# Fused attention, gated product and sine product on one core: the sine stages in another order

## The chip, the cores and the metric

The kernel runs on one core of a Trainium2 chip. The metric is the device time of one execution in microseconds (us); the time of a kernel is the median of its runs. Five engines with one instruction queue each work side by side: PE (TensorE: matmuls, and PEld, the weight loads that belong to them), DVE (VectorE), ACT (ScalarE), POOL (GpSimd) and SP (SyncE), which here issues the ordinary DMA transfers. An engine executes its instructions in the order in which they stand; where one waits for a semaphore, those behind it wait too.

## The reference

```python
x = attention(q, k, v)            # 4608 tokens x 512, chunks of 64 tokens, softmax within a chunk
x = ((x @ w1) * (x @ w2)) @ w3 @ w_o        # 512 -> 1024 -> 1024 -> 512
h = x @ w_in                      # 512 -> 2048
g = h * np.cos(h)
out = g @ w_out                   # 2048 -> 512, float32
```

All is float32. The kernel multiplies on the 16-bit path of PE: each operand is split in two float16 halves, and a product is made of three matmuls (high by high, low by high, high by low).

## The kernel before

The 4608 tokens are nine blocks of 512 (block 0 to block 8). Until about 730 us the kernel does attention and the gated product, and converts the weights of the sine part to halves that it keeps in DRAM. From there on it runs the **sine stages**, which the change is about: for each block `h_of` (first product, cosine, splitting of g) and `y_of` (second product).

Both products use Strassen's scheme in Winograd's form on 2x2 blocks: seven products in place of eight, with sums of blocks before and after. In `h_of` a block has four groups (`f_` 0 to 3). A group makes seven products (line 1296, 6 matmuls of 128x256 in each of two halves) in three PSUM tiles x, y and z; five PSUM banks serve these in turn. ACT copies a finished PSUM tile to SBUF (`kept`, line 1305), and DVE adds another to it (`plus`, line 1311). That gives four quarters of h: c11 (name hm1), c22 (hv5), c12 (hm3) and c21 (hu2). `finish` makes h cos h of each: two DVE instructions that take off whole turns (1336, 1339), a sine on ACT (1342), a multiplication on DVE (1345). `part` splits a quarter into halves, one instruction on ACT (1317) and one on DVE (1320): these are the operands of the second product. Operands 0, 1 and 2 are c11, c12 and c22 themselves. Operands 5, 3, 4 and 6 are sums, made in this chain: c11 += c21 (operand 5), then c21 += c22 (operand 3), c22 += c11 (operand 4), c12 += c22 (operand 6). Of these `add`s the first and third run on DVE (1330); the second and fourth are, in blocks 0 to 7, transfers that add in flight, which POOL issues (line 1326, 64 in all, 256 KB each). The third add overwrites c22, which the second reads; operand 3 needs the second to have landed, operand 6 the fourth.

`y_of` makes seven terms (line 1393, 12 matmuls for each of the four groups of one term) in three PSUM tiles of their own (psyx, psyy, psyz); line 1408 (ACT) and 1414 (DVE) take them out, line 1420 stores. Each term has its own 1 MB of weights, which SP fetches (line 1261) into one of three buffers; each pair of half groups of `h_of` needs 896 KB fetched in the same way. The second product of block b is interleaved with the first of block b + 1.

The order on every queue comes from a planner (`Plan.order`). It walks through time with a cost per instruction (for instance 0.7 us for an add on DVE), and when an engine is free it takes, of the instructions that are ready, the one with the lowest priority number. A result is ready for another engine at its planned end plus a latency from the table LAT. A transfer ends, in the plan, when its bytes have passed at DMA_RATE behind all earlier ones, and 2.2 us later it has landed. Most instructions of a group of `h_of` have the priority `pr`, the group's start in an even pace; the terms of `y_of` have `prio + i * unit`, i being the term's place. Nothing of the plan is kept at run time but the order: the engines wait for semaphores.

Of the kernel before, what the change touches and what calls it, by code (L numbers as in the profile page):

```python
# [25 lines left out]


MM = 0.2155
LAT = {"PE": 0.35, "DVE": 0.4, "ACT": 0.4, "POOL": 0.5, "SP": 2.2}
DMA_RATE = 380e3  # L30
ROWS = 2.7
AHEAD = 5.0
SHARED = 0.8
ISSUE = {"DVE": 0.9, "ACT": 0.88}
# [25 lines left out]


class Op:
    __slots__ = ("n", "eng", "cost", "prio", "fn", "deps", "succ", "bufs", "allocs", "left", "ready", "start", "size", "alts", "many", "psum")


class Plan:
# [6 lines left out]
        self.ops = []  # L73
        self.touched = {}

    def op(self, eng, cost, prio, fn, r=(), w=(), size=0, after=()):

        o = Op()
        o.psum = any(b.pool is not None and b.pool.places[0][0] == "PS" for b in (x[0] if isinstance(x, tuple) else x for x in r))
        o.many = isinstance(eng, dict)  # L80
        if o.many:
            o.alts, eng = eng, None
        else:
            o.alts = {eng: cost}
        o.alts = {e: c * ISSUE.get(e, 1.0) for e, c in o.alts.items()}
        o.n, o.eng, o.cost, o.prio, o.fn, o.size = len(self.ops), eng, cost, prio, fn, size
        o.deps, o.succ, o.bufs, o.allocs = set(), [], [], []
        norm = [x if isinstance(x, tuple) else (x, None) for x in r], [x if isinstance(x, tuple) else (x, None) for x in w]

        def meets(p, q):  # L90
            return p is None or q is None or p == q

        for b, part in norm[0]:
            assert b.writers, f"{b.name} is read before it is written"
            o.deps.update(x for x, p in b.writers if meets(p, part))
        for b, part in norm[1]:
            o.deps.update(x for x, p in b.writers if meets(p, part))
            o.deps.update(x for x, p in b.readers if meets(p, part))
        for b, part in norm[0]:
            b.readers.append((o.n, part))  # L100
        for b, part in norm[1]:
            if b.first is None:
                b.first = o.n
                if b.pool is not None:
                    o.allocs.append(b)
            b.writers = [(x, p) for x, p in b.writers if not (part is None or p == part)] + [(o.n, part)]
            b.readers = [(x, p) for x, p in b.readers if not (part is None or p == part)]
        for b in {id(b): b for b, _ in norm[0] + norm[1]}.values():
            b.users += 1
            o.bufs.append(b)  # L110
            o.deps.add(b.first)
        o.deps.update(x.n for x in after)
        o.deps.discard(o.n)
        self.ops.append(o)
        return o

    def order(self):
# [9 lines left out]
        left = {}  # L127
# [14 lines left out]
        ends = {}  # L142
# [14 lines left out]
        while done < len(ops):  # L157
# [11 lines left out]
            for e in ENGINES:  # L169
                while pending[e] and pending[e][0][0] <= now + 1e-9:  # L170
                    _, prio, n = heapq.heappop(pending[e])
                    heapq.heappush(waiting[e], (prio, n))
                if free[e] > now + 1e-9 or not waiting[e]:
                    continue
                if e == "SP" and dma > now + AHEAD:
                    heapq.heappush(wakes, dma - AHEAD)
                    continue
                aside, got = [], None
                while waiting[e]:
                    x = heapq.heappop(waiting[e])  # L180
                    o, taken, where = ops[x[1]], [], []
                    if o.start is not None:
                        continue
                    for b in o.allocs:
                        found = place(b, taken)
                        if found is None:
                            break
                        where.append((b, found[0]))
                        taken.append(found[1])
                    else:  # L190
                        got = o
                        for b, k in where:
                            b.place = k
                            if b.pool.queue:
                                b.pool.line.pop()
                        live += taken
                        break
                    aside.append(x)
                for x in aside:
                    heapq.heappush(waiting[e], x)  # L200
                if got is None:
                    continue
                o = got
                o.start, o.eng, o.cost = now, e, o.alts[e]
                if e == "DVE":
                    if not o.psum:
                        o.cost += SHARED * max(0.0, port - now)
                    on_psum = o.psum
                elif e == "POOL" and not o.size:
                    if free["DVE"] > now and not on_psum:  # L210
                        o.cost += SHARED * (free["DVE"] - now)
                    port = now + o.cost
                order.append(o)
                free[e] = now + o.cost
                end = now + o.cost
                if o.size:
                    dma = max(dma, now + o.cost) + o.size / DMA_RATE
                    end = dma
                heapq.heappush(wakes, free[e])
                for s in o.succ:  # L220
                    s.left -= 1
                    there = end if list(s.alts) == [e] and not o.size else end + LAT["SP" if o.size else e]
                    s.ready = max(s.ready, there)
                    if not s.left:
                        for a in s.alts:
                            heapq.heappush(pending[a], (s.ready, s.prio, s.n))
                        heapq.heappush(wakes, s.ready)
                for b in o.bufs:
                    left[id(b)] -= 1
                    ends[id(b)] = max(ends.get(id(b), 0.0), end + LAT["SP" if o.size else e])  # L230
                    if not left[id(b)] and b.pool is not None:
                        heapq.heappush(frees, (ends[id(b)], id(b), b))
                        heapq.heappush(wakes, ends[id(b)])
                done += 1
# [24 lines left out]
def fused_kernel(  # L259
# [33 lines left out]
    scale = 1.0 / math.sqrt(D)  # L293
    KB = 1024

    R0, R1, C0, C1, A0, A1, A2, A3, I0, I1, I2, I3, I4, I5, F0, Y1, Y0 = 0.9, 10.9, 16.5, 27.6, 60.0, 6, 70.0, 10.6, 240.5, 10.0, 28.1, 430.0, 5.6, 11.6, 8.4, 16.0, 8.0

    const = ctx.enter_context(tc.tile_pool(name="const", bufs=1))
    sb = ctx.enter_context(tc.tile_pool(name="sb", bufs=1))
# [157 lines left out]
    with tc.manual_schedule():  # L457
# [819 lines left out]
        def h_of(bl):  # L1277
# [8 lines left out]
            for f_ in range(K2 // 4):  # L1286
# [36 lines left out]
                def add(a, b, way, pr=pr):  # L1323
                    if way:
                        def f():
                            nc.gpsimd.dma_start(a.ap, b.ap, accum_op=ALU.add)
                        op("POOL", 1.2, pr, f, r=[a, b], w=[a], size=2 * P * 2 * KB)
                    else:
                        def f():
                            nc.vector.tensor_tensor(out=a.ap, in0=a.ap, in1=b.ap, op=ALU.add)  # L1330
                        op("DVE", 0.7, pr, f, r=[a, b], w=[a])
# [35 lines left out]
                plus(z, c21)  # L1367
                finish(0, 1, c21)
                way = [bl < NB - 1 and i in (1, 3) for i in range(4)]
                add(c11, c21, way[0])  # L1370
                add(c21, c22, way[1])
                part(5, c11)
                add(c22, c11, way[2])
                part(3, c21)
                add(c12, c22, way[3])
                part(4, c22)
                part(6, c12)

        def y_of(bl):
            tg, last = gh.pop(bl), bl == NB - 1  # L1380
            prio = start_h[bl] + (8 * pair + 20.0 if bl == 0 else period) + Y0
            unit, iy = period / 8, hsc[bl][2]
            x, y, z = (Buf(ps_y[n], f"psy{n}{bl}") for n in "xyz")

            def multiply(ps, a, b, i, more=False):
                w = fetch(bl, b, prio + i * unit - Y1)
                for f_ in range(4):
# [7 lines left out]
                                        start=(not more and f_ == 0 and n == 0 and j == 0 and m == 0), stop=(f_ == 3 and n == 1 and m == 2), skip_group_check=True,  # L1395
                                    )
                    at = prio + i * unit + f_ * unit / 8
                    if last and i in (0, 1, 3):
                        at = prio + (f_ - 4) * 8.0 + i
                    op("PE", 6 * MM, at, f, r=[tg[a, f_], w], w=[ps])  # L1400

            def two(a):
                return a.rearrange("p (j e) -> p j e", j=2)
# [21 lines left out]
            multiply(y, 1, 1, 1)  # L1425
            plus(y, c11, 1)
            store(c11, 0, 0, 1)
            multiply(x, 4, 4, 2, True)
            c21 = kept(x, "u2", 2)
            multiply(z, 5, 5, 3)  # L1430
            multiply(x, 3, 3, 4, True)
            c22 = kept(x, "v5", 4)
            plus(z, c22, 4)
            store(c22, 1, 1, 4)
            multiply(x, 6, 2, 5, True)
            c12 = kept(x, "m3", 5)
            store(c12, 0, 1, 5)
            multiply(z, 2, 6, 6, True)
            plus(z, c21, 6)
            store(c21, 1, 0, 6)  # L1440


        warm = Buf(ps_mm0, "warm")
# [65 lines left out]
```

## Time and profile before

| | |
|---|---|
| median of 3 runs | 1465.75 us (1462.08 to 1469.79) |
| the profiled execution | 1461.54 us |
| its span, first to last instruction | 1459.5 us |
| PE, share of the span | 94% |
| DVE, ACT, POOL | 80%, 66%, 15% |
| DMA, mean | 190 GB/s |

A busy PE is not a PE at its peak: its matmuls overlap, and their ends are modelled. Of an engine's row the number in square brackets is the idle time just before the instruction, with what ended it. The sine stages end with the program. In them a matmul of 128x256 follows the one before it after about 0.11 us if nothing holds it (13.11 us for 120 of them in the last group of rows below).

### The profile page before, as it was taken

The page shows a single profiled execution, that of the slowest core. Times are in us where ns is not written, and L with a number is a line of the kernel's source. Part 1 is how long each engine was busy: PE and PEld are TensorE (multiplying, and loading weights), DVE is VectorE, ACT ScalarE, POOL GpSimd, SP SyncE. Part 2 cuts the span into 40 slices and gives each one's busy share as a digit, 9 for nine tenths or more (in the row PEclk, how much of TensorE's full clock was granted, in tenths as well). Part 3 has the DMA queues.
Part 4 walks back from the last instruction along what each step waited for, and adds up shares of the span by engine and source line. Part 5 has one row for each costly group of instructions (what it writes and reads, how often), then busy time and mean ns, then how long its engine had stood idle before and what let it go on. Part 6 is the DMA issues. An engine that isn't in the chain of part 4 may idle for free. (4 is left out here: it accounts for less than half of the span.)

```text
span 1459.5 us, 32138 instructions
## 1 busy us (share of the span) xinstructions
PE 1378.7 (94%) x12984; PEld 1104.1 (76%) x12984; DVE 1172.3 (80%) x2015; ACT 958.2 (66%) x2090; POOL 224.2 (15%) x193
## 2 busy tenths in 40 slices
PE   5789999999999999999999898999898999999998
PEld 3356767777786868686878787888786888878887
DVE  8789787459989657895589898898878897978893
ACT  4788776769876769886377565656555564655552
POOL 0000114113641212531200000001000000000000
PEclk7999999999999999999999999999999999999999
DMA  9951582237777317635145787868585968777634
GB/s 317 270 113 36 159 275 52 74 76 235 191 232 224 77 54 218 178 91 199 76 154 179 251 262 236 271 222 249 171 302 167 302 195 269 219 248 238 225 131 146
DMA packets 196629, 276.83 MB, mean 190 GB/s; under 512 B 121216, under 2 KB 151936, under 8 KB 187264
## 3 DMA queue, kind: packets, MB, share of 16 engines
q1 hardware_dynamic: 187264, 257.99, 54.9%
q0 software_dynamic: 9216, 16.78, 6.5%
q8 instruction: 102, 1.67, 0.5%
q14 instruction: 47, 0.39, 0.1%
HBM read 224.40 MB, written 33.55 MB: 177 GB/s over the span
## 5 line engine op out<-in xcount | busy, mean ns | idle before, releaser
L978 PE MATMUL ps<-XHL,W 128*128 128x256 f16 x3024 | 347.1, 273 | 6.2 <-ACT RES L485 5.0
L1296 PEld LDWEIGHTS <-ATT 128*128 128x128 f16 x3024 | 297.1, 98 | 51.8 <-issue 14.7
L978 PEld LDWEIGHTS <-W 128*128 128x128 f16 x3024 | 292.6, 98 | 45.5 <-issue 7.4
L1393 PE MATMUL ps<-CONV,W 128*128 128x256 f16 x2304 | 278.0, 275 | 24.7 <-DVE W L1320 9.5
L1393 PEld LDWEIGHTS <-W 128*128 128x128 f16 x2304 | 225.6, 98 | 57.5 <-DVE W L1320 11.9
L1296 PE MATMUL ps<-XHL,ATT 128*128 128x256 f16 x1632 | 198.6, 274 | 6.2 <-ACT WG L1305 2.2
L1342 ACT ACTIVATE RES<-RES,quarter 128x512 f32<-128x512 f32 x144 | 102.9, 717 | 98.0 <-DVE RES L1339 97.8
L485 ACT ACTIVATE RES<-ps,smalls 128x512 f32<-128x512 f32 x126 | 87.2, 699 | 55.4 <-PE ps L978 50.4
L998 DVE SCALAR_TENSOR_TENSOR RES<-ps,smalls,RES 128x512 f32<-128x512 f32 x108 | 80.1, 746 | 45.0 <-ACT RES L485 25.4
L1088 PE MATMUL ps<-WG 128*128 128x512 f16 x288 | 109.2, 379 | 0.0
L1090 PE MATMUL ps<-WG 128*128 128x512 f16 x288 | 109.1, 379 | 0.0
L1089 PE MATMUL ps<-WG 128*128 128x512 f16 x288 | 109.1, 379 | 0.0
L1296 PE MATMUL ps<-WG,ATT 128*128 128x256 f16 x768 | 96.0, 274 | 4.8 <-ACT WG L1305 3.3
L751 ACT ACTIVATE ATT<-ps,SMALL 128x64 f32<-128x64 f32 x288 | 85.8, 328 | 21.4 <-DVE SMALL L746 19.0
L1013 POOL TENSOR_TENSOR WG<-RES,WG 128x512 f16<-128x512 f32 x46 | 58.6, 1277 | 258.5 <-DMA ATT<-in_v_dram 152.3
L1317 ACT ACTIVATE W<-WG,smalls 128x512 f16<-128x512 f32 x99 | 68.4, 713 | 37.2 <-DMA WG<-WG 24.8
L1393 PE MATMUL ps<-CONV,WG 128*128 128x256 f16 x720 | 88.1, 274 | 1.5 <-ACT CONV L1408 0.8
L1296 PE MATMUL ps<-RES,ATT 128*128 128x256 f16 x624 | 79.1, 273 | 0.9 <-ACT WG L1305 0.9
L1393 PEld LDWEIGHTS <-WG 128*128 128x128 f16 x720 | 70.4, 98 | 10.8 <-issue 1.2
L1320 DVE SCALAR_TENSOR_TENSOR W<-WG,smalls,W 128x512 f16<-128x512 f32 x99 | 71.7, 746 | 6.0 <-ACT W L1317 5.8
L662 DVE SCALAR_TENSOR_TENSOR XHL<-XHL,smalls 128x512 f16<-128x512 f32 x84 | 68.6, 837 | 8.2 <-ACT XHL L659 7.9
L481 ACT COPY ATT<-ps 128x512 f32<-128x512 f32 x108 | 61.3, 598 | 16.7 <-PE ps L767 13.0
(213 smaller groups left out, 2346.9 us busy)
## 6 DMA issues: line engine op xcount, KB each, us to landing
ATT<-win_dram SPq DMA_DIRECT2D x72, 896.0 KB, 6.8
CONV<-wout_dram SPq DMA_DIRECT2D x63, 1024.0 KB, 7.2
CONV<-in_moe_w_in_dram SPq DMA_DIRECT2D x32, 512.0 KB, 5.9
CONV<-in_moe_w_out_dram SPq DMA_DIRECT2D x32, 512.0 KB, 6.3
ATT<-in_v_dram SPq DMA_DIRECT2D x144, 64.0 KB, 2.5
u_dram<-TMP SPq DMA_DIRECT2D x36, 256.0 KB, 3.7
XHL<-u_dram SPq DMA_DIRECT2D x9, 1024.0 KB, 7.9
out_dram<-CONV SPq DMA_DIRECT2D x36, 256.0 KB, 6.9
```

The costliest lines, as they stand in the source:

```text
L485: nc.scalar.activation(dst, src, AF.Copy, scale=s)
L662: nc.vector.scalar_tensor_tensor(d.ap[:, :, 1], ap(x), scale[1], d.ap[:, :, 0], ALU.mult, ALU.subtract)
L751: nc.scalar.activation(probs()[:, b, a], scores()[:, a, b], AF.Exp, scale=scale, bias=mb.ap[:, 1, a, b : b + 1], accum_out=zb.ap[:, b, a : ...
L978: nc.tensor.matmul(ps.ap[:, p * half : (p + 1) * half], w12[j, g].ap[:, b, w_, c, p * P : (p + 1) * P], t[a].ap[:, c, u_], start=(not more ...
L998: nc.vector.scalar_tensor_tensor(b.ap, ps.ap, inv[1], b.ap, ALU.mult, ALU.add)
L1088: nc.tensor.matmul(ps.ap, wh.ap[:, kk, 0, ns], g[:, 0], start=(kk == 0), stop=False)
L1089: nc.tensor.matmul(ps.ap, wh.ap[:, kk, 0, ns], g[:, 1], start=False, stop=False)
L1090: nc.tensor.matmul(ps.ap, wh.ap[:, kk, 1, ns], g[:, 0], start=False, stop=(kk == K1 - 1))
L1296: nc.tensor.matmul(ps.ap[:, p * half : (p + 1) * half], wins[p].ap[:, b, k, w_], t[a].ap[:, k, u_], start=(not more and p == 0 and k == 0 ...
L1320: nc.vector.scalar_tensor_tensor(d.ap[:, 1], hs.ap, sg[1], d.ap[:, 0], ALU.mult, ALU.subtract)
L1342: nc.scalar.activation(r.ap, r.ap, AF.Sin, bias=quarters[side], scale=(2 * side - 1) * TURN)
L1393: nc.tensor.matmul(ps.ap[:, j * 256 : (j + 1) * 256], g[:, u_, n, j * P : (j + 1) * P], w.ap[:, 2 * f_ + n, w_], start=(not more and f_ == ...
```

## The change

Three things change, all in the order of instructions; no instruction is added or taken away, and no tile changes its size.

The planner's latencies: after an adding transfer its table has 5.5 us where it had 2.2. A multiplication of `y_of` is planned 2 us (SLACK) after its operand is ready (0 in the last block).

In `h_of` the adds and the operands made of them get a priority of their own, `late`, 6.5 of 7 units after the start of the group, and 8 us (LAG) more behind each add that is a transfer. Operand 3 moves ahead of the third add.

In `y_of` the seven terms run in the sequence of operands 0, 1, 5, 4, 3, 2, 6; before, it was 0, 1, 4, 5, 3, 6, 2. Their weights are fetched in that order, and the results leave in another order. The constant YU is the old `period / 8` rounded.

```diff
-LAT = {"PE": 0.35, "DVE": 0.4, "ACT": 0.4, "POOL": 0.5, "SP": 2.2}
+LAT = {"PE": 0.35, "DVE": 0.4, "ACT": 0.4, "POOL": 0.5, "SP": 2.2, "ADD": 5.5}
+LAG = 8.0
+SLACK = 2.0
...
-                    there = end if list(s.alts) == [e] and not o.size else end + LAT["SP" if o.size else e]
-                    s.ready = max(s.ready, there)
+                    there = end if list(s.alts) == [e] and not o.size and e != "SP" else end + LAT["ADD" if o.size and e == "POOL" else e]
+                    s.ready = max(s.ready, there + (0.0 if e in s.alts else s.slack))
...
-                add(c11, c21, way[0])
-                add(c21, c22, way[1])
-                part(5, c11)
-                add(c22, c11, way[2])
-                part(3, c21)
-                add(c12, c22, way[3])
-                part(4, c22)
-                part(6, c12)
+                late = pr + 6.5 * unit
+                add(c11, c21, way[0], late)
+                add(c21, c22, way[1], late)
+                part(5, c11, late)
+                late += LAG * way[1]
+                part(3, c21, late)
+                add(c22, c11, way[2], late)
+                late += LAG * way[2]
+                add(c12, c22, way[3], late)
+                part(4, c22, late)
+                part(6, c12, late + LAG * way[3])
...
-            unit, iy = period / 8, hsc[bl][2]
+            unit, iy = YU, hsc[bl][2]
...
-                    if last and i in (0, 1, 3):
+                    if last and i < 3:
...
-                    op("PE", 6 * MM, at, f, r=[tg[a, f_], w], w=[ps])
+                    op("PE", 6 * MM, at, f, r=[tg[a, f_], w], w=[ps], slack=0.0 if last else SLACK)
...
-            multiply(x, 4, 4, 2, True)
-            c21 = kept(x, "u2", 2)
-            multiply(z, 5, 5, 3)
+            multiply(z, 5, 5, 2)
+            multiply(x, 4, 4, 3, True)
+            c21 = kept(x, "u2", 3)
...
-            multiply(x, 6, 2, 5, True)
-            c12 = kept(x, "m3", 5)
-            store(c12, 0, 1, 5)
-            multiply(z, 2, 6, 6, True)
-            plus(z, c21, 6)
-            store(c21, 1, 0, 6)
+            multiply(z, 2, 6, 5, True)
+            plus(z, c21, 5)
+            store(c21, 1, 0, 5)
+            multiply(x, 6, 2, 6, True)
+            c12 = kept(x, "m3", 6)
+            store(c12, 0, 1, 6)
```

Up to the fetch of the third weights of the second product of block 0 every queue holds the same rows in the same order. Two places show what moves then. The names are those of SBUF regions (W, WG, RES, XHL, TMP, CONV, ATT) and PSUM banks (ps).

**DVE, block 4, from the `plus` that completes c11 of group 3.** Before, the queue goes on from that row (the first below) with work on operands of earlier groups:

```order
L1311 SCALAR_TENSOR_TENSOR WG<-ps_76,smalls,WG 128x512
L1320 SCALAR_TENSOR_TENSOR W_67<-W_67,smalls 128x512 x2
L1320 SCALAR_TENSOR_TENSOR W_67<-RES,smalls,W_67 128x512
L1320 SCALAR_TENSOR_TENSOR W_67<-WG,smalls,W_67 128x512
L1330 TENSOR_TENSOR W_67<-W_67,RES 128x512
L1345 TENSOR_TENSOR WG<-WG,RES 128x512
L1336 TENSOR_SCALAR RES<-WG 128x512
L1339 SCALAR_TENSOR_TENSOR RES<-RES,WG 128x512
L1320 SCALAR_TENSOR_TENSOR WG<-W_67,smalls,WG 128x512
```

The DVE half of operand 0 of that group, which is made of this very c11 (a row of line 1320), stands 56 instructions behind its `plus`. In the changed kernel `part` is line 1323, `plus` 1314, the adds 1333, the steps of `finish` 1339, 1342 and 1348. The `plus` and the first step of `finish` stand just ahead of these rows:

```order
L1348 TENSOR_TENSOR WG<-WG,RES 128x512
L1333 TENSOR_TENSOR WG<-WG 128x512
L1342 SCALAR_TENSOR_TENSOR RES<-RES,WG 128x512
L665 SCALAR_TENSOR_TENSOR RES<-TMP,smalls,RES 128x2x256
L665 SCALAR_TENSOR_TENSOR XHL<-XHL,smalls 128x2x256
L1323 SCALAR_TENSOR_TENSOR W_67<-WG,smalls,W_67 128x512
L1323 SCALAR_TENSOR_TENSOR WG<-WG,smalls 128x512
L1323 SCALAR_TENSOR_TENSOR W_67<-WG,smalls,W_67 128x512
L1348 TENSOR_TENSOR WG<-WG,RES 128x512
L669 TENSOR_TENSOR XHL<-XHL 128x2x256
L665 SCALAR_TENSOR_TENSOR XHL<-XHL,smalls 128x2x256
L1323 SCALAR_TENSOR_TENSOR W_67<-WG,smalls,W_67 128x512
```

The last row is the same operand 0, now 13 instructions behind its `plus`. In blocks 1 to 7 this distance was 40 to 67 and is 9 to 15; in block 8 it was 14 and is 6.

**ACT, block 7, up to the copy of the PSUM tile x of group 1 that frees it for its last product.** Before, the two rows of line 1317 in a row split operands 3 and 4 of group 3 of block 6, and the next row of line 1305 is that copy:

```order
L1305 ACTIVATE WG<-ps_7817,smalls 128x512
L1342 ACTIVATE RES<-RES,quarter_95 128x512
L1317 ACTIVATE WG<-RES,smalls 128x512
L1317 ACTIVATE WG<-W_67,smalls 128x512
L1305 ACTIVATE WG<-ps_7817,smalls 128x512
L1342 ACTIVATE RES<-RES,quarter_96 128x512
L1408 ACTIVATE CONV<-ps_781,smalls 128x512
```

In the changed kernel (`kept` is line 1308, `part` 1320, the sine 1345) four rows of `part` stand there:

```order
L1308 ACTIVATE WG<-ps_7817,smalls 128x512 x2
L1345 ACTIVATE RES<-RES,quarter_96 128x512
L1345 ACTIVATE RES<-RES,quarter_95 128x512
L1320 ACTIVATE W_67<-W_67,smalls 128x512
L1320 ACTIVATE W_67<-RES,smalls 128x512
L1320 ACTIVATE W_67<-W_67,smalls 128x512
L1320 ACTIVATE W_67<-WG,smalls 128x512
L1308 ACTIVATE WG<-ps_7817,smalls 128x512
```

They split operand 6 of group 3 of block 6, operands 1 and 5 of group 0 and operand 0 of group 1 of block 7; operands 3 and 4 of block 6 now stand far ahead of them.

## Rows read from the trace of the kernel before

**Rows 1.** Page, part 1: busy us (share of the span) xinstructions.

```profile
PE 1378.7 (94%) x12984; PEld 1104.1 (76%) x12984; DVE 1172.3 (80%) x2015; ACT 958.2 (66%) x2090; POOL 224.2 (15%) x193
```

**Rows 2.** Windows of 50 us: busy us of each engine, PEclk, DMA share, GB/s.

```profile
900.00:950.00 50.00, 47.39 (x416) 41.29 (x415) 43.10 (x71) 29.76 (x46) 4.30 (x5) 0.97 0.89 288
...
1100.00:1150.00 50.00, 43.84 (x384) 38.08 (x384) 41.59 (x70) 27.70 (x43) 3.95 (x5) 0.97 0.67 215
...
1200.00:1250.00 50.00, 47.58 (x418) 41.33 (x417) 41.11 (x68) 27.66 (x44) 4.30 (x5) 0.97 0.83 274
...
1300.00:1350.00 50.00, 50.00 (x451) 44.37 (x449) 39.85 (x65) 28.60 (x44) 4.32 (x5) 0.98 0.82 257
```

**Rows 3.** Waits of PEld, 750 to 1459.5 us: total us, times, longest us.

```profile
PEld L1393 <- DVE W L1320: 11.9, 11, 1.9
PEld L1393 <- ACT W L1317: 10.7, 6, 4.6
```

**Rows 4.** Waits of PE in the same stretch.

```profile
PE ps L1296 <- ACT WG L1305: 6.4, 4, 3.0
PE ps L1393 <- ACT CONV L1408: 4.5, 3, 2.9
PE ps L1393 <- DMA CONV<-wout_dram: 2.5, 2, 1.3
PE ps L1296 <- DVE WG L1311: 1.5, 1, 1.5
PE ps L1296 <- ACT RES L1305: 1.3, 2, 0.8
PE ps L1296 <- DVE W L1311: 1.1, 1, 1.1
```

**Rows 5.** Line 1326, the adding transfers: who waited (us, times), time to landing.

```profile
  ACT W L1317: 63.8, 26
  DVE WG L1330: 21.5, 9
...
DMA to landing us min/median/max: 3.2/5.2/10.6
```

**Rows 6.** Timeline 1283 to 1298 us: start, us, engine line op, [idle before <-releaser].

```profile
1283.85 1.64 SPq L1261 DMA_DIRECT2D CONV<-wout_dram  x2
...
1284.61 0.86 POOL L1326 DMA_DIRECT2D RES<-W  x1 [8.74 <-DVE WG L1330]
...
1295.21 0.72 ACT L1317 ACTIVATE WG<-RES,smalls 128x512 f16<-128x512 f32 x1 [4.05 <-DMA RES<-W]
...
1297.29 0.81 PE L1296 MATMUL ps<-WG,ATT 128*128 128x256 f16 x6 [2.97 <-ACT WG L1305]
```

**Rows 7.** Timeline of DVE, 1086.2 to 1129 us: one operand of block 4.

```profile
1086.31 0.75 DVE L1311 SCALAR_TENSOR_TENSOR WG<-ps,smalls,WG 128x512 f32<-128x512 f32 x1 [0.45 <-PE ps L1296]
...
1126.90 2.08 DVE L1320 SCALAR_TENSOR_TENSOR W<-WG,smalls,W 128x512 f16<-128x512 f32 x3 [4.15 <-ACT W L1317]
```

**Rows 8.** Timeline of all engines, 1086 to 1129 us: ACT and PE at that operand.

```profile
1126.15 1.95 ACT L1317 ACTIVATE W<-WG,smalls 128x512 f16<-128x512 f32 x3 [5.57 <-DMA WG<-WG]
...
1127.54 0.28 PE L1393 MATMUL ps<-CONV,W 128*128 128x256 f16 x1 [4.29 <-ACT W L1317]
```

**Rows 9.** Timeline of all engines, 1408 to 1424 us: the same operand of block 8.

```profile
1408.25 0.75 DVE L1311 SCALAR_TENSOR_TENSOR W<-ps,smalls,W 128x512 f32<-128x512 f32 x1
...
1418.49 0.75 DVE L1320 SCALAR_TENSOR_TENSOR W<-W,smalls 128x512 f16<-128x512 f32 x1
...
1422.69 1.47 PE L1393 MATMUL ps<-CONV,W 128*128 128x256 f16 x12
```

**Rows 10.** Chain in order of time from 1420 us: start, us, what.

```profile
1424.82 13.11 PE ps L1393 x120
...
1437.96 0.70 ACT CONV L1408
...
1444.18 0.70 ACT CONV L1408
```

More of the change, by code (lines that the diff above doesn't have):

```diff
@@ L62 @@
 class Op:
-    __slots__ = ("n", "eng", "cost", "prio", "fn", "deps", "succ", "bufs", "allocs", "left", "ready", "start", "size", "alts", "many", "psum")
+    __slots__ = ("n", "eng", "cost", "prio", "fn", "deps", "succ", "bufs", "allocs", "left", "ready", "start", "size", "alts", "many", "psum", "slack")
 class Plan:
@@ L74, in __init__, with op @@
         self.touched = {}
-    def op(self, eng, cost, prio, fn, r=(), w=(), size=0, after=()):
+    def op(self, eng, cost, prio, fn, r=(), w=(), size=0, after=(), slack=0.0):
         o = Op()
+        o.slack = slack
         o.psum = any(b.pool is not None and b.pool.places[0][0] == "PS" for b in (x[0] if isinstance(x, tuple) else x for x in r))
@@ L229, in order @@
                     left[id(b)] -= 1
-                    ends[id(b)] = max(ends.get(id(b), 0.0), end + LAT["SP" if o.size else e])
+                    ends[id(b)] = max(ends.get(id(b), 0.0), end + LAT["ADD" if o.size and e == "POOL" else e])
                     if not left[id(b)] and b.pool is not None:
@@ L294, in fused_kernel @@
     KB = 1024
-    R0, R1, C0, C1, A0, A1, A2, A3, I0, I1, I2, I3, I4, I5, F0, Y1, Y0 = 0.9, 10.9, 16.5, 27.6, 60.0, 6, 70.0, 10.6, 240.5, 10.0, 28.1, 430.0, 5.6, 11.6, 8.4, 16.0, 8.0
+    R0, R1, C0, C1, A0, A1, A2, A3, I0, I1, I2, I3, I4, I5, F0, Y1, Y0, YU = 0.9, 10.9, 16.5, 27.6, 60.0, 6, 70.0, 10.6, 240.5, 10.0, 28.1, 430.0, 5.6, 11.6, 8.4, 16.0, 8.0, 9.05
     const = ctx.enter_context(tc.tile_pool(name="const", bufs=1))
```

## The prediction

> **What bounds the kernel now.** The page comes first: PE is busy for 94% of the span [rows 1], so nearly every microsecond in which a matmul waits is lost to the end, and no other engine fills its time. The change leaves everything ahead of the sine stages in place, so only these are read, from 750 us on. The table by windows shows that DVE works 40 to 43 of 50 us there, ACT 28 to 30 [rows 2]: no second engine is full, but DVE has only a sixth of its time to spare. Then the waits of PE and of its weight loads. The second product (line 1393) waits for the two halves of its operands: 11.9 us for DVE and 10.7 for ACT [rows 3]. The first product (line 1296) waits for PSUM tiles to be copied out, 6.4 + 1.5 + 1.3 + 1.1 = 10.3 us in the four largest rows, and the second for its own tiles 4.5 and for fetched weights 2.5 [rows 4]. The granted clock stands at 0.97 in three windows and 0.98 in a fourth [rows 2]; each holds a short stretch at the lower of the two levels behind a stall. That costs 50 x (0.03 + 0.03 + 0.03 + 0.02) = 5.5 us. In all 22.6 + 10.3 + 7.0 + 5.5 = 45.4 us of the sine stages are not matmuls at full pace. This is the pool from which a new order can take.
>
> Why do these waits arise? Two patterns are to be seen.
>
> First, a queue is held up by an add that has not landed. SP issued two 1 MB fetches at 1283.85, POOL an adding transfer at 1284.61; ACT's `part` stood at the head of its queue until 1295.21, 10.6 us after the issue, 4.05 us of it idle; the copy of a PSUM tile stood two places behind, and PE waited 2.97 us for it [rows 6]. The same landing took between 3.2 and 10.6 us, median 5.2, and ACT and DVE waited for the largest groups of them 63.8 and 21.5 us [rows 5]. The plan allowed 2.2 beyond its own count of bytes.
>
> Second, DVE makes the operands long after their quarter of h is there. In block 4, group 3, the `plus` of c11 starts at 1086.31 and the DVE half of operand 0 ends with the second of three instructions of the row that starts at 1126.90, at about 1128.3 [rows 7]: 42 us, with 56 instructions between. ACT there had waited 5.57 us for a landing and PE 4.29 for ACT [rows 8]. In block 8, which has no adding transfers and 14 instructions between, the same path takes from 1408.25 to 1419.24, 11.0 us, and PE takes up the operand 3.5 us after it is done [rows 9].
>
> **The change part by part.** No instruction is added or removed, so busy times stay; the terms are the four waits above.
>
> *Operands of the second product, 22.6 us.* In the new order operand 0 of group 3 stands 13 instructions behind its `plus` in place of 56. At the 0.79 us per instruction of block 8 (11.0 / 14) the path is 10.2 us; with one wait as long as the 5.57 us in it, 15.8. PE comes to it 198 matmuls after the last one of the product that it is made from (318 in block 4 before); at 13.11 / 120 = 0.109 us each [rows 10] that is 21.6 us. So the operand is there 6 to 11 us early, although PE comes 13 us sooner than it did. Operand 4 of the same group, the second one on which PE waited, stands 27 instructions behind its last `plus` in place of 46 to 64 in blocks 1 to 6, 21.3 us, and PE comes after some 340 matmuls, 37 us in place of 32; the longest landing, 10.6, fits into the 14 instructions that now stand between the first add and the third (11.1 us). I take 1.5 us as what stays. The bounds are 0 and 10 (the waits that have a landing in them, nearly half).
>
> *Copies of PSUM for the first product, 10.3 us.* The 6.4 us for ACT are of the kind shown with a `part` ahead of a copy. ACT's `part` of operand 3 now stands 10 of its instructions behind the first add, before 6, and 9.1 us of matmuls lie between against 7.2; only landings near the longest still hold it up, by 1 to 2 us. The three smaller rows, 3.9 us, have products that follow each other into one tile with 18 matmuls, 2 us, between. That distance does not change, and I leave them: 4 us stay. Bounds 0 and 10.3.
>
> *Second product's own tiles and weights, 7.0 us.* The end stays as it is: the last two products into x follow each other there too, and PE stands for the copies of 0.70 us at 1437.96 and 1444.18 [rows 10], about 0.8 us each, 1.6 us. Of the two waits for weights the one in block 2 goes, since a fetch in the blocks 1 to 7 now has 20 us of matmuls or more between its buffer coming free and its use; the one in block 0 moves to the next fetch, which has 48 matmuls in place of 60, and grows from 1.3 to 2.6. The last fetch of block 8 has 48 in place of 60 too: up to 1.3 more. Sum 5.5; bounds 3 and 8. In exchange the tile x of one block is taken up by the next after 60 matmuls, 6.5 us, where 150 lay between. A copy of 0.70 us behind an ACT that is held up for 5.57 [rows 8] just fits, so I cost it at nothing; without that cover it would be about 0.5 us in each of 8 blocks, 4 us.
>
> *The clock, 5.5 us.* The low stretches stand behind the stalls. Where these go the clock stays up; I keep one of four, 1.4. Bounds 0 and 4.
>
> *Queues.* SP has the same transfers; two fetches and two stores of a block change places, and from block 2 on every half-group fetch has 10 us of matmuls or more between the release that it waits for and its use, where the shortest had 6.5. POOL has the same 64 adds. DVE gets less time per block: with 33 us less over eight blocks its share rises from some 83% to 87%, still below PE's.
>
> What stays is 1.5 + 4 + 5.5 + 1.4 = 12.4 us, so 45.4 - 12.4 = 33.0 us go. The profiled execution took 1461.5 us: 1428.5. The median of the runs lies 4.2 us above that execution; fewer waits for landings should narrow this, and I add half. Forecast: **1430 us**.
>
> **What a page says against it.** The adds landed after 3.2 to 10.6 us, median 5.2 [rows 5]. The Trainium skill, "DMA: Bandwidth & Descriptors", section "Anatomy of one DMA — SWDGE (gpsimd) path", fits a transfer that POOL issues as about 2.0 us plus its bytes at 436 GB/s, which for 256 KB makes an estimate of 2.6 us. By that rule the old 2.2 us were about right and 5.5 only hold rows back, and the sum would be nothing gained; the trace agrees with it at the shortest landing alone. The same page's section "Queues, rings and completion order" says that the transfer engines take packets from the queues in turn, by which an add beside one fetch should about double, an estimate of some 6.4 us from the shortest row; the add behind two fetches at 1284.61 took 10.6 [rows 6], so the constant 5.5 falls short of it. That is the first rival.
>
> **The rivals.**
> *Landings stay the limit.* The plan's constant does not know when two fetches lie ahead of an add. If half of the operand and copy waits stay (16.5 us), with 5.5 and half of the clock's, 2.8, then 24.8 stay, 20.6 go: 1440.9, and 2 more: 1443. For it: slow landings of 8 to 10 us are frequent. Against it: the distances behind an add have grown on both queues, and operands have 6 us or more in hand.
> *Slower: the cover of operand 0.* The new order gives up 120 matmuls, 13 us, of distance between the product and its use in blocks 1 to 7. Were the 13 instructions to take up two of the longest landings, 10.2 + 2 x 10.6 = 31.4 us, PE would stand 9.8 us in each of seven blocks: 69 more, 1499. It decides from a path of 21.6 us on, and cancels the gain from about 27. For it: 42 us were measured on that path. Against: 56 instructions stood in it, and block 8 shows 11 for 14.
> *Nothing changes.* The order is new and the waits form again elsewhere, with some 40 us as before: 1464. The operand distances, a quarter of what they were, speak against it.
>
> **How the numbers follow.** 0.70 for the forecast (own range 1418 to 1442), 0.20 for late landings, 0.05 each for nothing and for slower. About 0.5%, 7 us, is what a measurement of this kernel can tell from no change. The lower end of the range: all terms at their low bound leave 3 us, 42 go, 1419, and a few less in a quick run: 1415. The upper: 10 + 10.3 + 8 + 4 + 4 = 36 stay, 9 go, 1452, and 3 for the median: 1455. Faster 0.90, same 0.05, slower 0.05.
>
> **What would show it.** Right: the weight loads of the second product wait under 5 us for DVE and ACT together (22.6 now); the first product's largest wait for ACT, 6.4 us, falls under 3; no window but the first and last of the sine stages has a clock under 1.00; the idle time of ACT and DVE for adding transfers falls by more than half although their landings take as long. Wrong: a new largest row in the waits of PE, above all for operand 0 at the start of each block's second product, for the tile x, or for a fetch; or PE's waits unchanged with other names.

## The result, and the profile after

The changed kernel takes **1415.95 us** (median of 4 runs, 1415.73 to 1418.52) against 1463.91 of the kernel before beside it (4 runs, 1458.93 to 1469.79): a ratio of 0.9675, 95% interval 0.9635 to 0.9714. Forecast were 1430 us in a range of 1415 to 1455: the time lies 1 us above the lower end of that range, and 2 below the 1418 that the forecast gave as the lower end of its own case. From profile to profile the span fell from 1459.5 to 1413.8 us, 45.7. Not only the median fell: the runs of the kernel before lie 11 us apart, those of the changed one 3.

The page after, its parts on the span and on busy time, answers to [rows 1]:

```profile
span 1413.8 us, 32143 instructions
...
PE 1369.1 (97%) x12984; PEld 1105.2 (78%) x12984; DVE 1173.2 (83%) x2015; ACT 956.7 (68%) x2090; POOL 226.1 (16%) x193
```

DVE and ACT have the same busy time as before. PE's idle time (span less busy) fell from 80.8 to 44.7 us, and its busy time by 9.6, for two reasons that rows show. At the lower clock a full window holds fewer matmuls: 451 from 1300 to 1350 us in [rows 2], 461 in a window below. And the modelled end of a matmul covers the start of the stall behind it: the two last stalls in the changed kernel are 1.6 us in the rows of PE and 1.9 in those of its weight loads (both shown below). Idle and busy time make the 45.7. The table by windows, which answers to [rows 2], shows where the idle time went:

```profile
750.00:800.00 50.00, 47.41 (x398) 38.54 (x397) 49.24 (x90) 35.95 (x60) 6.36 (x7) 1.00 0.63 190
800.00:850.00 50.00, 49.58 (x453) 44.04 (x451) 49.35 (x82) 32.92 (x52) 4.29 (x5) 1.00 0.85 270
...
900.00:950.00 50.00, 50.00 (x460) 44.74 (x459) 49.48 (x83) 32.42 (x52) 4.31 (x5) 1.00 0.82 254
...
1100.00:1150.00 50.00, 50.00 (x461) 44.83 (x459) 45.22 (x74) 29.70 (x47) 4.60 (x5) 1.00 0.78 246
...
1350.00:1400.00 50.00, 48.45 (x444) 43.13 (x442) 33.37 (x53) 20.48 (x31) 0.00 (x0) 1.00 0.49 168
```

461 matmuls fit into 50 us now, 0.108 us each, with the granted clock (seventh figure behind the window) at 1.00; before, the full windows from 750 us on held 384 to 451, and five of them stood below 1.00, the four of [rows 2] and one at 0.99. DVE (third pair of figures) is now close to full as well, with 49.2 to 49.5 of 50 us from 750 to 950. These are all the rows of PE's waits from 750 us on, which answer to [rows 4]:

```profile
PE ps L1399 <- ACT CONV L1414: 1.6, 2, 0.8
PE ps L1299 <- DVE RES L665: 1.2, 1, 1.2
PE ps L1399 <- DVE W L1323: 1.1, 1, 1.1
PE ps L1299 <- DVE W L1314: 0.4, 1, 0.4
PE ps L1299 <- DVE WG L1314: 0.3, 1, 0.3
```

The row of line 665 is no copy of PSUM: that line splits an operand of the first product. The waits of the weight loads answer to [rows 3]:

```profile
PEld L1299 <- issue: 3.1, 6, 1.3
PEld L1399 <- issue: 1.9, 2, 1.0
PEld L1399 <- DVE W L1323: 1.4, 1, 1.4
```

Those of line 1399 (before 1393) wait 1.4 us for DVE and not at all for ACT, where [rows 3] had 11.9 and 10.7 ("issue": the profile names no semaphore for the load; the two of line 1399 are the copies at the end, which the matmul row names). The adding transfers (line 1329, before 1326) answer to [rows 5]; who waited for them (us, times), and their time to landing:

```profile
  ACT W L1320: 16.7, 11
  ACT WG L1320: 9.7, 6
  DVE W L1333: 0.3, 1
...
DMA to landing us min/median/max: 3.2/6.0/10.6
```

They land no sooner than before, rather later (median 6.0 for 5.2). But DVE meets one only once, for 0.3 us, and of the 26 us that ACT still waits none shows up in PE's rows. Operand 0 of block 4, group 3, from its `plus` to its DVE half, and the matmuls that take it up, which answer to [rows 7] and [rows 8]: first the timeline of DVE, then that of PE.

```profile
1066.94 0.74 DVE L1314 SCALAR_TENSOR_TENSOR WG<-ps,smalls,WG 128x512 f32<-128x512 f32 x1
...
1075.16 0.75 DVE L1323 SCALAR_TENSOR_TENSOR W<-WG,smalls,W 128x512 f16<-128x512 f32 x1
```

```profile
1087.62 1.47 PE L1399 MATMUL ps<-CONV,W 128*128 128x256 f16 x12
```

The path takes 9.0 us where it took 42, and the operand is ready 11.7 us before PE comes to it. For operand 0 of group 3 in blocks 1 to 7 that time in hand is 6.6 to 14.1 us; before, it was -1.9 to 0.6 (negative where PE had begun on the half that ACT makes).

### The profile page after: what moved, and what is told of

Read it like the earlier page. It is cut to its first block, busy times and chain, and to the rows that moved or that the text cites. A ratio compares the mean times of both kernels' runs of the same rounds, so it can differ in the third digit from the quotient of the medians.

```text
span 1413.8 us, 32143 instructions
## 1 busy us (share of the span) xinstructions
PE 1369.1 (97%) x12984; PEld 1105.2 (78%) x12984; DVE 1173.2 (83%) x2015; ACT 956.7 (68%) x2090; POOL 226.1 (16%) x193
## 4 chain that ended last, share of the span: by engine, by line
PE 74%; DVE 15%; ACT 5%; DMA 4%; issue 2%; SPq 0%; ACTq 0%; DVEq 0%
PE ps L981 20%; PE ps L1399 20%; PE ps L1299 17%; PE ps L1091 3%; PE ps L1093 3%; PE ps L1092 3%; DVE W L1323 2%; PE ps L722 2%; PE ps L737 1%; PE ps L929 1%; DVE RES L1342 1%; DMA CONV<-in_moe_w_out_dram 1%; ACT ATT L754 1%; PE ps L785 1%; DVE RES L1339 1%
## 5 line engine op out<-in xcount | busy, mean ns | idle before, releaser
L1016 POOL TENSOR_TENSOR WG<-RES,WG 128x512 f16<-128x512 f32 x46 | 58.8, 1283 | 257.9 <-DMA ATT<-in_v_dram 150.6
L1320 ACT ACTIVATE W<-WG,smalls 128x512 f16<-128x512 f32 x102 | 71.2, 713 | 22.6 <-DMA WG<-WG 10.6
L1308 ACT ACTIVATE WG<-ps,smalls 128x512 f32<-128x512 f32 x76 | 51.1, 680 | 46.1 <-PE ps L1299 45.8
L1399 PE MATMUL ps<-CONV,WG 128*128 128x256 f16 x672 | 81.7, 273 | 0.0
```

The source lines that it names most:

```text
L1320: nc.scalar.activation(d.ap[:, 0], hs.ap, AF.Copy, scale=sg[1])
L1399: nc.tensor.matmul(ps.ap[:, j * 256 : (j + 1) * 256], g[:, u_, n, j * P : (j + 1) * P], w.ap[:, 2 * f_ + n, w_], start=(not more and f_ == ...
```

## The experiments

Two theories stood after the result. **Distance**: the operands come late because their instructions stand too far behind their sources, and the new places put them near. **Landing**: what delays operands and copies is that adds which have not landed stand at the heads of the queues of DVE and ACT, and the change only gives them time. A third, that the sequence of the terms or SLACK did it, stood beside them. Ratios are against runs of the kernel before taken beside each, with 95% intervals.

### One part alone, and one undone

**The new places alone** (`late` and LAG, put into the kernel before):

```diff
+LAG = 8.0
-                add(c11, c21, way[0])
-                add(c21, c22, way[1])
-                part(5, c11)
...
+                late = pr + 6.5 * unit
+                add(c11, c21, way[0], late)
+                add(c21, c22, way[1], late)
+                part(5, c11, late)
+                late += LAG * way[1]
...
```

> The kernel before with one part of the change: operands and adds of a group at the priority 'late', LAG behind each transfer; latency 2.2, no SLACK, old terms. In its order operand 0 of group 3 stands 8 to 12 DVE instructions behind its plus (40 to 67 before), with 198 matmuls of cover; the third add stands 10 behind the first as before. Theory 'distance' (operands come late because their instructions stand too far back): waits of line 1393's weight loads for DVE and ACT fall from 22.6 to under 4 us, 1425 to 1440 us. Rival 'landing' (the adds that have not landed hold the queues, and only planning with 5.5 helps): ACT still waits for landings 60 us or more, PE's waits stay over 25 us, 1445 us or more.

Measured: 1437.48 us, ratio 0.980 (0.977 to 0.983). Waits of the weight loads, all from 750 us on (line 1397 is the second product, 1297 the first):

```profile
PEld L1297 <- issue: 17.8, 16, 2.4
PEld L1397 <- issue: 4.1, 4, 1.7
PEld L1297 <- DMA ATT<-win_dram: 0.4, 1, 0.4
```

No operand is late, and the time lies in the range of "distance". But ACT and DVE still wait 67 us for landings, and the first product waits 17.8 us (the largest of the matmul rows behind it name ACT's copies). So 29 us come with the places, and about 20 are missing.

**The latency of 5.5 us alone:**

```diff
-LAT = {"PE": 0.35, "DVE": 0.4, "ACT": 0.4, "POOL": 0.5, "SP": 2.2}
+LAT = {"PE": 0.35, "DVE": 0.4, "ACT": 0.4, "POOL": 0.5, "SP": 2.2, "ADD": 5.5}
...
```

> The kernel before with the latency of 5.5 us after an adding transfer alone. In its order operand 0 stands 73 to 97 DVE instructions behind its plus, but PE takes it up only after some 680 matmuls (318 before). Theory 'distance': 91 instructions at 0.79 us are 72 us against 680 x 0.109 = 74 us of cover, no more in hand than before: 1448 to 1470 us. Rival 'landing': the queues no longer meet adds that have not landed, 1415 to 1435 us.

Measured: 1569.22 us, ratio 1.070 (1.067 to 1.073): neither theory's range, 103 us slower. PE's four largest waits:

```profile
PE ps L1296 <- ACT WG L1305: 23.9, 10, 3.4
PE ps L1393 <- ACT W L1317: 22.9, 9, 4.5
PE ps L1296 <- DMA ATT<-win_dram: 22.0, 14, 2.8
PE ps L1393 <- DVE W L1320: 14.1, 13, 2.0
```

A wait is new that neither the kernel before nor the changed one has in these rows: the first product for its fetched weights (ATT). In this order the buffer of such a fetch comes free 42 matmuls (4.6 us) before its next use in the median of blocks 1 to 7; before it was 138, in the changed kernel 135.

**The latency back at 2.2 us, the rest of the change kept:**

```diff
-LAT = {..., "SP": 2.2, "ADD": 5.5}
+LAT = {..., "SP": 2.2, "ADD": 2.2}
```

> The changed kernel with the latency after an adding transfer back at 2.2 us, all else kept. Operand 0 stands 7 to 18 DVE instructions behind its plus; the third add 10 behind the first (14 in the changed kernel), ACT's part of operand 3 6 behind (10). Theory 'distance': operands keep 6 us or more in hand, so within 6 us of the changed kernel, 1414 to 1422 us, though ACT waits for landings as long as before the change. Rival 'landing': most of the gain goes, 1440 us or more.

Measured: 1439.01 us, ratio 0.983 (0.977 to 0.989): 23 us of the gain are lost, close to the range of "landing". No operand of the second product is late; most of the loss stands before the first product, whose matmul rows name ACT's copies:

```profile
PEld L1299 <- issue: 32.8, 24, 4.4
```

The profiled execution took 1453.85 us, the slowest of four from 1433.48 on; so the row belongs to a loss of 38 us and not of 23 (3.1 in the changed kernel).

**The old places, the rest of the change kept:**

```diff
-                late = pr + 6.5 * unit
...
+                add(c11, c21, way[0])
+                add(c21, c22, way[1])
+                part(5, c11)
+                add(c22, c11, way[2])
+                part(3, c21)
...
```

> The changed kernel with the adds and operands back at their old priorities and in their old sequence; latency 5.5, SLACK and new terms kept. Operand 0 stands 81 to 97 DVE instructions behind its plus, with 690 matmuls of cover. Theory 'distance': 92 x 0.79 = 73 us against 75 us: operands are late again in most blocks, 1445 us or more. Rival 'landing', and the rival that the sequence of terms did it: 1416 to 1430 us.

Measured: 1581.64 us, ratio 1.079 (1.076 to 1.081). The direction is that of "distance", the size is not, and no operand is late: PE waits 53.2 us for the first product's fetched weights and 44.6 for one group of copies. Setting LAG to 0 in the changed kernel gives this very order, row for row on every engine, so this run stands for that too: with the latency at 5.5 us, `late` moves nothing by itself, and of the new places the 8 us behind a transfer are all that counts.

**Sequence of terms and SLACK.** The two parts that work together, without the other two (LAT with ADD and the new places are kept from the changed kernel):

```diff
-SLACK = 2.0
+SLACK = 0.0
...
-            multiply(z, 5, 5, 2)
-            multiply(x, 4, 4, 3, True)
+            multiply(x, 4, 4, 2, True)
+            multiply(z, 5, 5, 3)
...
```

> Latency 5.5 us and the new places together, without SLACK and with the old sequence of terms. Operand 0 stands 9 to 17 DVE instructions behind its plus, ACT's part of operand 3 stands 10 behind the first add as in the changed kernel. Theory 'both places and landing, the rest for nothing': 1415 to 1422 us. Rival 'the sequence and SLACK carry the last 20 us': 1430 us or more.

Measured: 1418.05 us, ratio 0.967 (0.963 to 0.970). And each taken out of the changed kernel by itself, the sequence first:

```diff
-            multiply(z, 2, 6, 5, True)
-            plus(z, c21, 5)
-            store(c21, 1, 0, 5)
-            multiply(x, 6, 2, 6, True)
+            multiply(x, 6, 2, 5, True)
...
+            multiply(z, 2, 6, 6, True)
+            plus(z, c21, 6)
+            store(c21, 1, 0, 6)
```

> The changed kernel with the old sequence of the seven terms (operands 0, 1, 4, 5, 3, 6, 2). PE comes to operand 4 after 252 matmuls (27 us) in place of 342; its DVE half stands 27 instructions behind its plus, 21 us. The cover should do: 1415 to 1421 us. Rival 'operand 4 is late again': line 1399's loads wait for DVE and ACT 10 us or more, 1428 us or more.

Measured: 1417.20 us, ratio 0.966 (0.963 to 0.969).

```diff
-SLACK = 2.0
+SLACK = 0.0
```

> The changed kernel with SLACK = 0, all else kept. The distances in its order are those of the changed kernel (operand 0 9 to 14 DVE instructions behind its plus, third add 14 behind the first). Theory 'landings alone': 1414 to 1420 us. Rival 'the 2 us planned behind an operand carry some of it': 1424 us or more.

Measured: 1417.27 us, ratio 0.965 (0.961 to 0.969). All three lie within about 2 us of the changed kernel; neither the sequence nor SLACK has an effect that these runs can tell from none.

### The landings taken out of an order

Here the order stays as it is, row for row; the transfer goes, and with it the wait for its landing. These kernels leave out the second and fourth adds and serve for their time alone.

```diff
-                            nc.gpsimd.dma_start(a.ap, b.ap, accum_op=ALU.add)
+                            nc.gpsimd.memset(a.ap[:, :1], 0.0)
```

**In the kernel with the latency back at 2.2 us (1439 us):**

> The kernel with the latency at 2.2 us (1439 us), its order of instructions kept, but each of the 64 adding transfers replaced by POOL setting one column of the same tile to zero: the second and fourth adds are left out, and their readers wait for POOL and for no landing. Theory 'a copy behind an add that has not landed' (the 23 us between that kernel and the changed one are waits for landings): 1412 to 1422 us, the waits of the first product's weight loads for 'issue' fall from 33 to under 6 us. Rival 'the order itself is worse' (distances between products and copies): 1432 us or more.

Measured: 1414.67 us, ratio 0.965 (0.962 to 0.968); the first product's weight loads wait 4.4 us for "issue" where they waited 32.8 in that slowest execution. All of the 23 us go with the transfers; without them this order takes no longer than the changed kernel does with them.

**In the kernel before:**

> The kernel before, order kept, with the 64 adding transfers replaced by POOL setting one column of the same tile to zero (second and fourth adds left out). It tells how much of the 45 us of waits comes from landings and how much from the distance of the operands. Theory 'both': the copies' waits go and the operands' waits shrink, since each late landing delays 56 instructions behind it: 1425 to 1445 us. Theory 'distance alone': 1445 us or more. Theory 'landing alone': 1412 to 1424 us, the waits of line 1393's weight loads for DVE and ACT under 3 us.

Measured: 1420.23 us, ratio 0.967 (0.964 to 0.970). The time is in the range of "landing alone", but its condition is missed: the waits of line 1393 for DVE and ACT come to 5.3 us, not under 3. Of its weight loads' waits these are the rows:

```profile
PEld L1393 <- DVE W L1320: 4.9, 4, 1.6
PEld L1393 <- issue: 2.6, 3, 1.0
PEld ps L537 <- DVE WG L1311: 0.7, 1, 0.7
PEld L1296 <- issue: 0.4, 2, 0.3
PEld L1393 <- ACT W L1317: 0.4, 1, 0.4
```

And operand 0 of block 4, group 3, in its timelines (DVE, then PE), 56 instructions behind its `plus` as before:

```profile
1070.53 0.75 DVE L1311 SCALAR_TENSOR_TENSOR WG<-ps,smalls,WG 128x512 f32<-128x512 f32 x1 [0.46 <-PE ps L1296]
...
1104.20 2.07 DVE L1320 SCALAR_TENSOR_TENSOR W<-WG,smalls,W 128x512 f16<-128x512 f32 x3
```

```profile
1105.04 0.27 PE L1393 MATMUL ps<-CONV,W 128*128 128x256 f16 x1
1105.66 1.05 PE L1393 MATMUL ps<-CONV,W 128*128 128x256 f16 x8 [0.35 <-DVE W L1320]
```

The path still takes 35 us (it ends with the second of the three instructions, at 1105.6) and the operand still comes at the last moment: PE waits 0.35 us for it, where it waited 4.29 [rows 8]. So the distance cost little by itself, 5.3 us of the 22.6 at most. It left nothing in hand, and a late landing went straight through to PE.

That experiment also takes 64 transfers off the DMA engines. **The same with as many bytes that nobody waits for:**

```diff
-                            nc.gpsimd.dma_start(a.ap, b.ap, accum_op=ALU.add)
+                            nc.gpsimd.memset(a.ap[:, :1], 0.0)
+                            n = beside.pop()
+                            nc.gpsimd.dma_start(spare[n], wout_dram[n % 7].rearrange("p k e -> p (k e)")[:, :1024])
```

> The kernel before, order kept; each adding transfer replaced by POOL setting one column of the tile to zero (second and fourth adds left out) and then issuing a transfer of 256 KB from DRAM to DRAM for which nobody waits. So 64 transfers of the same bytes stay beside the fetches, and the waits for their landing are gone. Theory 'waits for landings': 1412 to 1426 us, as without the transfers (1420). Rival 'the bytes themselves hold up the fetches': 1440 us or more.

Measured: 1422.87 us, ratio 0.970 (0.966 to 0.974). The kernel before gains 48 and 41 us in these two, against its own runs beside each (1467.73 and 1464.24). The fetches land as late beside these transfers as beside the adds; their medians from 750 us on, first in the kernel before, then here, then without any transfer of POOL:

```profile
CONV<-wout_dram SPq DMA_DIRECT2D x60, 1024.0 KB, 7.1
ATT<-win_dram SPq DMA_DIRECT2D x66, 896.0 KB, 6.6
...
CONV<-wout_dram SPq DMA_DIRECT2D x60, 1024.0 KB, 7.3
ATT<-win_dram SPq DMA_DIRECT2D x66, 896.0 KB, 6.7
...
CONV<-wout_dram SPq DMA_DIRECT2D x60, 1024.0 KB, 6.3
ATT<-win_dram SPq DMA_DIRECT2D x66, 896.0 KB, 6.1
```

So the bytes account for a small part of the gain at most.

**The same edit (POOL sets one column, no transfer) in the order made with the latency of 5.5 us alone (1569 us):**

> The order of the kernel with the latency of 5.5 us alone (1569 us), with the 64 adding transfers replaced by POOL setting one column of the same tile to zero (second and fourth adds left out). Theory 'the order itself costs': without landings it still takes 1540 us or more, the first product still waits for its fetched weights and for copies. Rival 'landings cost there too': 1430 us or less. Between: both.

Measured: 1550.81 us, ratio 1.056 (1.052 to 1.060). Here the order itself costs: 18 us of the 103 are landings, the rest is not.

### No adding transfer at all

```diff
-                way = [bl < NB - 1 and i in (1, 3) for i in range(4)]
+                way = [False for i in range(4)]
```

> The kernel before with all adds on DVE: no adding transfer, nothing left out, priorities and terms as before; the planner makes another order (operand 0 10 to 20 DVE instructions behind its plus). Theory 'landings alone': the waits go, but DVE gets 64 adds more, 64 x 0.60 = 38 us on 42 to 47 of 50 us: 49 of 50, so it becomes as full as PE, 1418 to 1440 us, ahead of the kernel before. Rival 'DVE bounds': 1450 us or more.

Measured: 1434.43 us, ratio 0.977 (0.974 to 0.980), some 34 us faster than before and 18 slower than the changed kernel. Two windows of it, and two of its three largest rows of PE's waits:

```profile
1000.00:1050.00 50.00, 49.41 (x452) 43.99 (x451) 49.32 (x81) 32.80 (x50) 0.00 (x0) 1.00 0.67 246
...
1200.00:1250.00 50.00, 48.96 (x444) 43.13 (x442) 49.18 (x80) 31.75 (x49) 0.00 (x0) 1.00 0.56 201
```

```profile
PE ps L1296 <- DVE WG L1311: 5.3, 7, 3.0
...
PE ps L1296 <- DVE RES L1311: 3.5, 6, 1.0
```

In the windows from 850 to 1350 us DVE is busy some 49.2 of 50 us and PE makes 444 to 452 matmuls per window in place of 461; the two rows of the first product are waits for `plus` on DVE. So the transfers are worth having where their landings are covered: they keep DVE from being a second bound. The order is another one here too, and what of the 18 us is due to that was not measured apart.

## Why the prediction was right, and where it was not

**Direction and mechanism.** The pool was the right one: waits of PE in the sine stages. That a late landing at the head of a queue makes them was read from [rows 6], and the order without landings shows that it makes nearly all of them: 1420 us without a single instruction moved, 1423 with as many bytes beside it. The signs that were named came: the weight loads wait 1.4 us for operands, no row of the first product for ACT is left, and ACT and DVE wait 26.7 us for landings where two rows of [rows 5] alone had 85.3. But the sum is some 14 us too slow, and the measured time is faster than the 1419 at which all of its terms were at their low bound; the range holds it by the few us that were added there. That it does is luck, the direction is not.

**The operand term: its size right, its second cause wrong.** 22.6 us were to shrink to 1.5, and 1.4 is measured; the path was worked out at 10.2 us and takes 9.0, the time in hand at 6 to 11 us and is 11.7. But the step "DVE makes the operands long after their quarter of h is there" was given as a cause beside the landings. By itself it is a small one: with 56 instructions between, and no landings, those waits are 5.3 us. What the new places do is to put 7 to 14 us in hand, which swallow a late landing.

**The copies: mis-sized for a wrong reason.** 4 us were to stay, since 18 matmuls between two products into one tile do not change. Two rows of 0.7 us together are measured (and 1.2 for the operand of line 665, which the prediction did not have), and with the landings out of the old order the first product's weight loads wait 0.4. The three small rows of 3.9 us went with the landings as well.

**Own tiles and weights: mis-sized.** 5.5 were to stay, 1.6 did, just the two copies at the end. No fetch is waited for. The fetch of block 0 that has 48 matmuls of cover was costed with the 7.8 us of the old one; but the old one had a second fetch issued 1.3 us behind it, and the new one, issued at 792.33 with none close behind, landed after 4.9 us, 2.7 before its use. The last fetch of block 8 landed after 5.5 us, 1.4 before its use. The tile x, with 60 matmuls between two blocks, has no row either, as forecast.

**The clock, and the rest.** 1.4 us of low clock were to stay; no window from 750 to 1400 us is under 1.00. Of the 12.4 us to stay 4.6 did, that is 7.8 too many. The pool of 45.4 us was also some 5 short of what went (45.7 + 4.6): the smaller rows left out of it come to 2.7 us (0.7 and 0.5 for the first product, 1.0 for the second, 0.5 of clock). The rest, some 2 us, is not shown by a row of its own; the part of each stall that a matmul's modelled end covers, and a clock read in hundredths, would be of that size. The half of 4.2 us that was added for the median did not come: the medians of the changed kernel and its profiled run agree within 0.2 us.

**The queues.** DVE was to rise from some 83% to 87%. In the windows it is at 98 to 99% from 750 to 950 us and at 90 to 94% from there to 1250; the 83% came from the four windows of [rows 2], and others were fuller. PE stays full beside it, so it cost little here, but DVE is the next bound, as the kernel with all adds on DVE shows.

**The rivals.** Late landings did stay, with a median of 6.0 us, and by the Trainium skill, "DMA: Bandwidth & Descriptors", section "Queues, rings and completion order", a POOL add takes turns with SP's fetches packet by packet. The 6.4 us estimated from it were for one fetch: the adds of before with one fetch beside them took a median of 4.6 us, those with two or more 8.8 (last section). Nor is the plan's constant all that it allows, as the prediction read it: the planner counts 1.2 us for POOL and the bytes of the add and of the fetches ahead as well. By the planner of the kernel before, an add lands 4.8 to 9.0 us after its start, and 24 of the 64 landed later than planned, by up to 4.6 us and by 58.5 in all. By that of the changed kernel, with 5.5 us, it is 8.1 to 12.2, and 12 landed later, by up to 1.4 us and 8 in all. So late landings did not stay the limit, and the waits that remain on ACT no longer reach PE. The slower rival asked for a path of 21.6 us or more, and 9.0 came. A slower order was near all the same: one constant of the same change, alone, loses 103 us.

**What stays open:** why the planner, given the 5.5 us without LAG, makes an order with so little cover for the first product's fetches. What that order costs is shown, how it comes about was not tried.

## What to carry to other kernels

A plan that counts on a transfer sooner than it lands puts its readers at the heads of in-order queues, and everything behind them waits too. The median does not tell this: it was 5.2 us where the planner of the kernel before had 5.9, and yet 24 of 64 came late. So plan with the landing time that the trace shows under load, and give the readers a later place. To find out what such waits cost, keep the order and take the landing out of it: that told in two runs what no distance read from the order could. And parts of a change to a planner need not add up: the latency that brought 20 us with the new places cost 103 without them.

## What was not expected of the hardware

The landing of an adding transfer hangs on the fetches that SP issues around it, just behind it as well as ahead. In the trace of before, sorted by the fetches of 896 KB or 1 MB that were under way when the add started or were issued within 1 us behind it (as far as their landing is recorded): with none, 17 adds took 3.2 to 4.1 us (median 3.5); with one, 22 took 3.2 to 9.8 (4.6); with two or more, 25 took 5.4 to 10.6 (8.8). The profile after gives the same picture (medians 3.4, 3.9, 8.3). The slowest add, that of [rows 6], started behind one fetch alone, at 1284.61 us; the second of the two fetches in that row came 0.56 us behind it:

```profile
1285.17 0.32 SPq L1261 DMA_DIRECT2D CONV<-wout_dram  x1
```

So no single constant behind the counted bytes fits all three groups.
